# Strassen's seven block products in the last batch's second layer

## The chip, the core and the metric

The kernel runs on one core of one Trainium2 chip. The metric is the device time of one execution in microseconds, as the median of several runs; less is better. Engines are named as in the profile: PE is TensorE, PEld its weight loads, DVE is VectorE, ACT is ScalarE, POOL is GpSimd and SP is SyncE, which here only issues DMAs.

## The reference

Attention with normalised queries and keys feeds a two-layer network with a tanh GELU. The change touches only the last product, `g @ w_out`.

```python
q_n, k_n = rmsnorm(q, g_q), rmsnorm(k, g_k)          # (8, 12, 448, 64)
attn = softmax(q_n @ k_n.T / 8)
x = (attn @ v).transpose(0, 2, 1, 3).reshape(3584, 768)
h = x @ w_in                                         # w_in: 768 x 2048
g = 0.5 * h * (1 + tanh(c * (h + 0.044715 * h**3)))
out = g @ w_out                                      # w_out: 2048 x 768
```

## The kernel before

The 8 batches of 448 tokens go one after the other. For each batch the kernel does attention, then the first layer, and it mixes the second layer of the batches before into the attention of the next one, so that TensorE has work while ScalarE takes exponentials. The order in which instructions are written is the order in which each engine executes them; where one engine needs another's result, it waits on a semaphore. Nothing reorders them afterwards.

The **first layer** of a batch (`mm1_pair`, matmuls on L499) makes the 2048 hidden columns in 16 chunks of 128. Hidden values lie transposed: the tile `g` has 128 partitions (the place within a chunk), 16 chunks (`nf`), and 896 tokens, since two batches stand side by side. ScalarE applies the GELU from PSUM into `g` (L512), two chunks at a time and the last two chunks singly. PSUM is used as four pairs of banks that go round (`pair`, `give`): `s0`, `s1`, `t0`, `t1`.

The **second layer** goes by tiles of 128 tokens, 7 for two batches. Tiles 0 to 2 are taken after an even batch, tiles 3 to 6 after an odd one. For all but the last batch the matmuls (L442, `mm2_quarters`) are spread through the next batch's attention. After the last batch nothing is left to mix with, so `m2_parts` returns the calls of `mm2_last` (L465 to L487), which run on their own at the end: tiles 3 to 6, each in two blocks of 384 output columns, each block 16 matmuls of 128 x 128 weights by 384 columns that accumulate in one bank; the very last block is cut into two of 192 columns. Of each block ScalarE or VectorE copies the finished bank into `osb` (three buffers of 128 x 768 in `op`), and `store` issues two DMAs of 64 tokens each to the output, on SyncE's queue, the very last one on ScalarE's.

In the last batch the first layer runs with an empty plan beside it: `m1` has no entries, since there is no next batch to load or normalise. VectorE's last work ahead of it is the product `xT` (L408).

Of the kernel before, what the change touches and what calls it, by code (L numbers as in the profile page):

```python
# [8 lines left out]
F32 = mybir.dt.float32  # L9
BF16 = mybir.dt.bfloat16  # L10
I32 = mybir.dt.int32
AF = mybir.ActivationFunctionType
ALU = mybir.AluOpType
# [4 lines left out]
def kernel(  # L18
# [11 lines left out]
    nc = tc.nc  # L30
    B, H, S, D = q.shape
    assert (B, H, S, D) == (8, 12, 448, 64)
    d_model = H * D
# [4 lines left out]
    P = 128  # L38
    R = 64
    NT = S // R  # L40
    NCH = H // 4
    HP = H // 2
    nf = d_ff // 128
    HD = d_model // 2
# [5 lines left out]
    rawqk = ctx.enter_context(tc.tile_pool(name="rawqk", bufs=4))  # L50
    sqp = ctx.enter_context(tc.tile_pool(name="sqp", bufs=2))
    stp = ctx.enter_context(tc.tile_pool(name="stp", bufs=1))
# [3 lines left out]
    exq = ctx.enter_context(tc.tile_pool(name="exq", bufs=2))  # L56
    xp = ctx.enter_context(tc.tile_pool(name="xp", bufs=2))
    gp = ctx.enter_context(tc.tile_pool(name="gp", bufs=1))
    op = ctx.enter_context(tc.tile_pool(name="op", bufs=3))
# [11 lines left out]
    def pair(name):  # L71
        t = idle_pairs.pop(0)
        if not whole:
            idle_pairs.append(t)
        return t

    def give(t):
        if whole:
            idle_pairs.append(t)
# [29 lines left out]
    wout = wts.tile([128, nf, d_model], BF16)  # L109
# [6 lines left out]
    g = gp.tile([128, nf, 2 * S], BF16, tag="g", name="g")  # L116
# [56 lines left out]
    def total(b, c, n, hs=both, ts=slice(0, NT)):  # L173
        if b not in sss:
            sss[b] = smp.tile([P, NCH, 2, 2, NT], F32, tag="ss", name="ss")
        nc.vector.reduce_sum(  # L176
            sss[b][:, c, "qk".index(n), hs, ts], squares(b, c, n, hs, ts), axis=AX.X
        )
# [140 lines left out]
    def gain(b, c):  # L319
        nc.vector.tensor_scalar(kT[:, c], kT[:, c], gcol[:, 0:1], None, op0=ALU.mult)  # L320
# [98 lines left out]
    osbs = {}  # L419
    SYNC = mybir.DependencyInfo(mybir.DependencyClass.Sync, mybir.DependencyReason.DATA)  # L420

    def store(b, i, cols=slice(0, d_model), engs=(nc.sync, nc.sync)):
        for j in range(2):
            col = i * 128 + j * R
            r = ((b // 2) * 2 + col // S) * R
            engs[j].dma_start(
                out_v[col % S // R, r:r + R, cols], osbs[i][j * R:(j + 1) * R, cols]
            )

    def mm2_quarters(b, parts, p, f, copy=None):  # L430

        if p == 0 and f == 0:
            osbs["o"] = pair("o")
            for i, half in parts:
                if half == 0:
                    osbs[i] = op.tile([128, 2, HD], F32, tag="osb", name="osb").rearrange(
                        "p h d -> p (h d)")
        o = osbs["o"]
        for n, (i, half) in enumerate(parts):
            rs = slice((n ^ p) * R, (n ^ p) * R + R)  # L440
            for c in range(2):
                done = nc.tensor.matmul(  # L442
                    o[c * R:(c + 1) * R, n, :HD],
                    g[rs, f, i * 128 + c * R:i * 128 + (c + 1) * R],
                    wout[rs, f, half * HD:(half + 1) * HD],
                    start=(p == 0 and f == 0), stop=(p == 1 and f == nf - 1),
                )
                if p == 1 and f == 0 and n == 0 and c == 0:
                    tc.add_manual_dep(done.ins, osbs["turn"].ins.name, SYNC)
        if p == 0 and f + 1 == nf:  # L450
            osbs["turn"] = nc.sync.nop(nofuse=True)  # L451
            tc.add_manual_dep(osbs["turn"].ins, done.ins.name, SYNC)
        if p == 0 or f + 1 < nf:
            return
        if parts[0][0] == parts[1][0]:
            copy(osbs[parts[0][0]].rearrange("p (h d) -> p h d", h=2), o[:, :, :HD])
        else:
            for n, (i, half) in enumerate(parts):
                copy(osbs[i][:, half * HD:(half + 1) * HD], o[:, n, :HD])
        give(o)  # L460
        for i, half in parts:
            if half == 1:
                store(b, i)

    def mm2_last(i, lo, hi, f):  # L465

        last = hi == d_model and i == 6
        if f == 0:
            osbs["o"] = pair("o")
            if lo == 0:  # L470
                osbs[i] = op.tile([128, d_model], F32, tag="osb", name="osb")
        o, osb = osbs["o"][:, 0, :hi - lo], osbs[i]
        nc.tensor.matmul(  # L473
            o, g[:, f, i * 128:(i + 1) * 128], wout[:, f, lo:hi],
            start=(f == 0), stop=(f == nf - 1),
        )
        if f + 1 < nf:
            return
        if i < 6 and lo == 0 or i == 6 and not last:
            nc.scalar.copy(osb[:, lo:hi], o)  # L480
        else:
            nc.vector.tensor_copy(osb[:, lo:hi], o)
        give(osbs["o"])
        if i == 6:
            store(B - 1, i, slice(lo, hi), (nc.sync, nc.scalar if last else nc.sync))
        elif hi == d_model:
            store(B - 1, i)  # L487

    def mm1_pair(i, cs=range(HP), b=0, js=range(2)):

# [28 lines left out]

    def m2_parts(b):  # L520
        tiles = range(3) if b % 2 == 0 else range(3, 7)
        if b + 1 == B:
            q = HD // 2
            cuts = [(i, lo, lo + HD) for i in tiles for lo in (0, HD)]
            i, lo, hi = cuts.pop()
            cuts += [(i, lo, lo + q), (i, lo + q, hi)]
            return [
                lambda cut=cut, f=f: mm2_last(*cut, f) for cut in cuts for f in range(nf)
            ]
        order = [(i, half) for i in tiles for half in range(2)]  # L530
        if b == 0:

            order.sort(key=lambda t: t[1])
        return [
            lambda copy, n=n, p=p, f=f: mm2_quarters(b, order[n:n + 2], p, f, copy)
            for n in range(0, len(order), 2) for p in range(2) for f in range(nf)
        ]
# [56 lines left out]
    def plan(*entries):  # L594
        steps = {}
        for slot, *fns in entries:
            steps.setdefault(slot, []).extend(fns)
        return steps
# [63 lines left out]
    def gpsimd_waits(x):  # L662

        nc.gpsimd.tensor_copy(mark, x)  # L664
# [57 lines left out]
    def first_two(steps, m2):  # L722
# [3 lines left out]
        for step in steps.split():  # L726
# [91 lines left out]
    m2 = []  # L818
# [25 lines left out]
            )    , m2)  # L844
    begun = 2
    for b in range(1, B):
        m1, side, ends = [], [], []
        if b + 1 < B:

            if (b, NCH - 1) in ess:  # L850
                m1.append((0, lambda: gpsimd_waits(ess[b, NCH - 1][:1, 0, :1])))
            for c in range(NCH):
                if b == 1 and c + 1 == NCH:
                    m1 += [(0, lambda: total(2, 2, "q")), (0, lambda: total(2, 2, "k")),
                           (6, lambda: rsqrt_last(2))]
                m1 += [(6 if (b, c) == (1, NCH - 1) else 0,
                        lambda c=c: normed_both(b + 1, c, nc.gpsimd)),
                       (4 * c + 4, lambda c=c: transposed(b + 1, c))]
            m1 += [(9, lambda: gain(b + 1, 0)), (14, lambda: gain(b + 1, 1))]
        if b + 2 < B:  # L860
            m1 += [(4, lambda: loads(b + 2, 1)), (8, lambda: loads(b + 2, 2))]
            for c, at in ((0, 4), (1, 9)):
                for i, (n, a) in enumerate((n, a) for n in "qk" for a in range(2)):
                    m1.append((at + i, lambda c=c, n=n, a=a: squared(b + 2, c, n, a)))
                m1 += [(at + 2, lambda c=c: total(b + 2, c, "q")),
                       (at + 4, lambda c=c: total(b + 2, c, "k"))]
            for n in "qk":
                m1.append((13, lambda n=n: square(b + 2, 2, n, nc.gpsimd)))
                side.append((0, lambda n=n: total(b + 2, 2, n)))
        if b + 1 < B:  # L870
            side.append((0, lambda: gain(b + 1, 2)))
        m1 = plan(*m1)
        for f in range(nf):
            if f + 1 == nf:
                for j in range(2):
                    mm1_pair(f // 2, range(HP), b, range(j, j + 1))
            elif f % 2:
                mm1_pair(f // 2, late if f // 2 < begun else range(HP), b)
            for fn in m1.get(f, ()):
                fn()  # L880
        m2 += m2_parts(b)
        if b + 1 == B:
            for fn in m2:
                fn()
            break
        nc.scalar.preload_act_table_set(EXP_SET)
        if b + 2 < B:
            ends.append(lambda: rsqrt(b + 2))
            side.append((0, lambda: load_v(b + 2, 0, HP)))
            if b + 3 < B:  # L890
                side.append((1 if b % 2 else 2, lambda: loads(b + 3, 0)))
        begun = attention(b + 1, m2, plan(*side), ends)
# [30 lines left out]
```

## Time and profile before

| what | value |
|---|---|
| median of 3 runs (lowest, highest) | 396.68 us (396.26, 397.37) |
| span of the profiled execution, first to last instruction | 394.7 us |
| time of the profiled execution outside its span | not in the profile; the median of the runs is 2.0 us above the span |
| granted TensorE clock | 1.000 |
| TensorE busy | 387.2 us (98%) |
| ScalarE, VectorE, GpSimd busy | 277.2, 252.3, 125.9 us |
| last batch's second layer on TensorE | 369.8 to 390.8 us from the span's start |

A row of the timeline gives start and length in us, engine, line, operation, result<-sources, shapes and count; in brackets the idle time of the engine ahead of it and what ended that. In a row with a count, the length reaches from the first start to the last end. A group row gives the busy time in us, the mean of one in ns, and the idle time before. Matmuls are pipelined: a matmul's row begins when it starts, and the next one starts before it has ended, so the rate is read from starts.

### The profile page before, as it was taken

How to read it: one execution, taken by the hardware profiler on the slowest of the kernel's cores; microseconds unless marked ns; L12 is line 12 of the kernel's file. 1: busy time of each engine (PE TensorE's matmuls, PEld its weight loads, DVE VectorE, ACT ScalarE, POOL GpSimd, SP SyncE). 2: the span in 40 equal slices, each digit the busy share in tenths (PEclk: the TensorE clock that was granted, in tenths of full speed). 3: DMA queues.
4: the chain of work that ended last, by engine and by line, in shares of the span. 5: the costliest groups of instructions: out<-in, count | busy, mean ns of one | idle time of the engine just before them, and what ended most of it. 6: DMA issues, size and time to landing. Idle time of an engine off the chain costs nothing.

```text
span 394.7 us, 12736 instructions
## 1 busy us (share of the span) xinstructions
PE 387.2 (98%) x5673; PEld 247.8 (63%) x5673; DVE 252.3 (64%) x386; ACT 277.2 (70%) x348; POOL 125.9 (32%) x105
## 2 busy tenths in 40 slices
PE   8989999999999999999999999999999999999996
PEld 7455557855666558855666557865666557865564
DVE  5999539997699267954599367963499505980010
ACT  6995389566995689847997579857898259854300
POOL 5995501865205540092203640073301800000000
PEclk9999999999999999999999999999999999999999
DMA  8999995899823958159731948249522611220033
GB/s 270 245 238 221 204 180 170 282 195 277 187 67 67 263 68 218 44 140 227 160 89 42 219 112 214 71 92 267 82 63 63 117 25 42 60 64 2 0 82 80
DMA packets 65594, 54.36 MB, mean 138 GB/s; under 512 B 37380, under 2 KB 60548, under 8 KB 65540
## 3 DMA queue, kind: packets, MB, share of 16 engines
q1 hardware_dynamic: 53184, 41.48, 40.7%
q0 software_dynamic: 12128, 11.80, 19.3%
q8 instruction: 44, 0.72, 0.7%
q10 hardware_dynamic: 228, 0.28, 0.2%
q14 instruction: 10, 0.08, 0.1%
HBM read 45.61 MB, written 11.01 MB: 143 GB/s over the span
## 4 chain that ended last, share of the span: by engine, by line
PE 93%; ACT 5%; DVE 1%; issue 0%; DVEq 0%; ACTq 0%
PE s L499 21%; PE t L442 19%; PE t L499 15%; PE s L442 12%; PE s L382 5%; ACT ex L337 4%; PE s L333 4%; PE t L333 3%; PE s L473 3%; PE t L382 3%; PE t L473 2%; PE o L271 2%; PE tp L296 1%; PE o L382 1%; PE hh L499 1%
## 5 line engine op out<-in xcount | busy, mean ns | idle before, releaser
L499 PEld LDWEIGHTS <-win 128*128 128x128 bf16 x768 | 74.4, 98 | 70.8 <-issue 2.7
L442 PEld LDWEIGHTS <-g 64*64 64x64 bf16 x3072 | 97.3, 107 | 33.1 <-SPq L451 2.9
L337 ACT ACTIVATE ex<-s,shift 128x896 bf16<-128x896 f32 x101 | 97.8, 1012 | 4.3 <-PE s L333 2.4
L442 PE MATMUL t<-wout,g 64*64 64x384 bf16 x1792 | 90.0, 323 | 0.0
L499 PE MATMUL s<-xT,win 128*128 128x448 bf16 x438 | 88.3, 353 | 0.0
L176 DVE TENSOR_REDUCE ss<-sq 128x14 f32<-128x896 f32 (+3 forms) x45 | 44.3, 996 | 45.7 <-ACT sq L169 42.9
L337 ACT ACTIVATE ex<-t,shift 128x896 bf16<-128x896 f32 x67 | 66.4, 1014 | 5.8 <-PE t L333 3.0
L512 ACT ACTIVATE g<-s 128x896 bf16<-128x896 f32 (+1 forms) x41 | 34.0, 835 | 48.5 <-PE s L499 48.5
L499 PE MATMUL t<-xT,win 128*128 128x448 bf16 x318 | 64.7, 353 | 0.0
L442 PE MATMUL s<-wout,g 64*64 64x384 bf16 x1280 | 64.6, 323 | 0.1
L512 ACT ACTIVATE g<-t 128x896 bf16<-128x896 f32 (+1 forms) x30 | 24.8, 829 | 26.3 <-PE t L499 26.3
L333 PE MATMUL s<-qT,kT 64*64 64x448 bf16 x404 | 37.3, 353 | 1.7 <-ACT ex L337 1.5
L664 POOL COPY mark<-es 1x1 bf16<-1x1 bf16 x5 | 0.9, 177 | 116.9 <-DVE es L356 116.9
L278 POOL TENSOR_TENSOR nrmk<-rawk,rinv 128x896 bf16<-128x896 f32 (+1 forms) x21 | 34.6, 1649 | 6.3 <-DVE o L245 6.3
L278 POOL TENSOR_TENSOR nrmq<-rawq,rinv 128x896 bf16<-128x896 f32 (+1 forms) x21 | 34.6, 1645 | 4.6 <-ACT rinv L208 3.4
L333 PEld LDWEIGHTS <-kT 64*64 64x64 bf16 x672 | 23.2, 106 | 14.5 <-issue 6.1
L171 POOL TENSOR_TENSOR sq<-rawq 128x896 f32<-128x896 f32 (+1 forms) x9 | 13.7, 1522 | 51.4 <-DMA rawq<-in_q_dram 24.6
L382 PEld LDWEIGHTS <-vb 64*64 64x64 bf16 x672 | 22.5, 107 | 8.4 <-issue 0.3
L400 DVE STREAM_TRANSPOSE rb<-rc 128x896 f32<-128x896 f32 x24 | 26.7, 1111 | 0.8
L333 PE MATMUL t<-qT,kT 64*64 64x448 bf16 x268 | 23.8, 351 | 0.3 <-ACT ex L337 0.2
L359 DVE TENSOR_TENSOR e<-ex 128x896 bf16<-128x896 bf16 x33 | 20.0, 606 | 6.2 <-ACT ex L337 6.2
L382 PE MATMUL s<-ex,vb 64*64 64x448 bf16 x420 | 22.6, 349 | 0.0
(107 smaller groups left out, 390.0 us busy)
## 6 DMA issues: line engine op xcount, KB each, us to landing
out_dram<-osb SPq DMA_DIRECT2D x54, 192.0 KB, 2.7
rawq<-in_q_dram SPq DMA_DIRECT2D x23, 448.0 KB, 4.6
rawk<-in_k_dram SPq DMA_DIRECT2D x23, 448.0 KB, 5.5
vb<-in_v_dram POOLq DMA_DIRECT2D x8, 672.0 KB, 6.8
wout<-in_moe_w_out_dram POOLq DMA_DIRECT2D x2, 1536.0 KB, 23.1
win<-in_moe_w_in_dram POOLq DMA_DIRECT2D x6, 256.0 KB, 10.5
win<-in_moe_w_in_dram POOLq DMA_DIRECT2D x4, 384.0 KB, 12.4
kT<-nrmk SPq DMA_TRANSPOSE x19, 3.9
```

What stands on the lines that cost most here:

```text
L171: eng.tensor_mul(sq, raw, raw)
L176: nc.vector.reduce_sum(sss[b][:, c, "qk".index(n), hs, ts], squares(b, c, n, hs, ts), axis=AX.X)
L278: eng.tensor_mul(nrms[n, b, c][:, ts].rearrange("p t a d -> p a t d"), raws[n, b, c][:, :, ts], root[:, :, ts].to_broadcast([P, 2, m, D]),)
L333: nc.tensor.matmul(sc[r * R:(r + 1) * R, a, :S], kT[rs, c, t, r], qT[b][rs, c, :, r], start=True, stop=True,)
L337: nc.scalar.activation(ex[:, t], sc[:, :, :S], AF.Exp, scale=scale, bias=shift)
L359: nc.vector.tensor_add(e2, ex[:, t - 1], ex[:, t])
L382: nc.tensor.matmul(o[r][a * D:(a + 1) * D], vb[b % 2][rs, 2 * c + a, i] if what else ones[rs], es[i][rs, a], start=(i == 0), stop=(i == n ...
L400: nc.vector.transpose(rb.rearrange("p r s -> p (r s)"), rc.to_broadcast([128, 2 * S // 32, 32]))
L442: done = nc.tensor.matmul(o[c * R:(c + 1) * R, n, :HD], g[rs, f, i * 128 + c * R:i * 128 + (c + 1) * R], wout[rs, f, half * HD:(half + 1) ...
L473: nc.tensor.matmul(o, g[:, f, i * 128:(i + 1) * 128], wout[:, f, lo:hi], start=(f == 0), stop=(f == nf - 1),)
L499: nc.tensor.matmul(h[j][:, :S] if type(h) is list else h[:, j, :S], win[:, c, f * 128:(f + 1) * 128], xT[b][:, c], start=(c == 0), stop=(c ...
L512: nc.scalar.activation(g[:, 2 * i + lo:2 * i + js[-1] + 1, (b % 2) * S:(b % 2 + 1) * S], h[:, lo:js[-1] + 1, :S], AF.Gelu_apprx_tanh)
```

## The change

The last second layer is done for two pairs of token tiles, (3, 4) and (5, 6). For each pair the product is a 2 x 2 block product: two token tiles by two halves of the hidden chunks (8 each, `nh`) times two halves of the hidden chunks by two halves of the output columns (384 each). Strassen's scheme needs seven block products of 8 matmuls in place of eight:

- the five sums of blocks of `w_out` are formed once by VectorE (`weight_sums`), each in two parts of 128 x 1536 bf16, into buffers that the loads of raw q and k and the squares no longer need;
- the five sums of blocks of `g` are formed for each pair by VectorE (`token_sums`): that for product 6 whole (128 x 1024), the four others in halves (128 x 512), of which the second halves need the last chunks of `g`;
- the products accumulate in PSUM where they can (product 5 onto product 3, product 2 onto product 4, in the first pair product 7 onto product 1), and VectorE and ScalarE form the four output blocks from them in `osb`. `s34` is the sum of products 3 and 4; `m1` is product 3, copied by ScalarE so that VectorE reads one bank only.

`mm2_last` and its place in `m2_parts` go. The new part of the diff:

```diff
+    half_cols = (slice(0, HD), slice(HD, d_model))
+    nh = nf // 2
+    def w_block(i, j, f, n=1):
+        return wout[:, i * nh + f:i * nh + f + n, half_cols[j]]
+    W_SUMS = {"1": ((0, 0), (1, 1), ALU.add), "3": ((0, 1), (1, 1), ALU.subtract),
+              "4": ((1, 0), (0, 0), ALU.subtract), "6": ((0, 0), (0, 1), ALU.add),
+              "7": ((1, 0), (1, 1), ALU.add)}
+    def weight_sums(m, part):
+        x, y, op = W_SUMS[m]
+        n = nh // 2
...
+        nc.vector.tensor_tensor(
+            t, w_block(*x, part * n, n), w_block(*y, part * n, n), op=op)
+        wsum[m, part] = t
+    G_SUMS = {"1": ((0, 0), (1, 1), ALU.add), "2": ((1, 0), (1, 1), ALU.add),
+              "5": ((0, 0), (0, 1), ALU.add), "6": ((1, 0), (0, 0), ALU.subtract),
+              "7": ((0, 1), (1, 1), ALU.subtract)}
+    def g_block(qd, i, j, f, n=1):
+        t = qd[i]
+        return g[:, j * nh + f:j * nh + f + n, t * 128:(t + 1) * 128]
+    def token_sums(qd, m, part=None):
...
+        x, y, op = G_SUMS[m]
+        lo, n = (0, nh) if part is None else (part * nh // 2, nh // 2)
+        nc.vector.tensor_tensor(
+            asum[qd, m][:, lo:lo + n], g_block(qd, *x, lo, n), g_block(qd, *y, lo, n), op=op)
+    def product(qd, m, o, start, lo=0, hi=HD):
+        for f in range(nh):
+            nc.tensor.matmul(
+                o[:, lo:hi], g_of(qd, m, f), w_of(m, f)[:, lo:hi],
+                start=start and f == 0, stop=f == nh - 1, skip_group_check=True,
+            )
+    def quad_of_products(qd, last):
+        c1, c2 = half_cols
+        for i in qd:
+            osbs[i] = op.tile([128, d_model], F32, tag="osb", name="osb")
+        o1, o2 = osbs[qd[0]], osbs[qd[1]]
...
+        x, y = bank("x"), bank("y")
+        product(qd, "3", x, True)
+        product(qd, "4", y, True)
+        nc.scalar.copy(m1, x)
+        nc.vector.tensor_add(s34, y, m1)
+        product(qd, "5", x, False)
+        nc.scalar.copy(o1[:, c2], x)
+        nc.vector.tensor_sub(o1[:, c1], s34, x)
+        give(one["x"])
+        store(B - 1, qd[0], c2)
+        product(qd, "2", y, False)
+        nc.scalar.copy(o2[:, c1], y)
+        nc.vector.tensor_sub(o2[:, c2], s34, y)
+        give(one["y"])
+        store(B - 1, qd[1], c1)
+        z = bank("z")
+        product(qd, "1", z, True)
+        nc.vector.tensor_add(o2[:, c2], z, o2[:, c2])
+        if last:
+            nc.vector.tensor_add(o1[:, c1], z, o1[:, c1])
+        w = bank("w")
+        product(qd, "6", w, True)
+        nc.vector.tensor_add(o2[:, c2], w, o2[:, c2])
+        give(one["w"])
+        store(B - 1, qd[1], c2, (nc.sync, nc.scalar if last else nc.sync))
+        cuts = ((bank("v"), 0, HD // 2), (z, HD // 2, HD)) if last else ((z, 0, HD),)
+        for o, lo, hi in cuts:
+            product(qd, "7", o, last, lo, hi)
+            nc.vector.tensor_add(o1[:, lo:hi], o[:, lo:hi], o1[:, lo:hi])
+            store(B - 1, qd[0], slice(lo, hi), (nc.sync, nc.scalar if hi == HD else nc.sync))
+        give(one["z"])
...
+    quads = ((3, 4), (5, 6))
...
+        if b + 1 == B:
+            for i, (m, part) in enumerate((m, part) for m in W_SUMS for part in range(2)):
+                m1.append((2 + i, lambda m=m, part=part: weight_sums(m, part)))
+            for qd in quads:
+                m1.append((9, lambda qd=qd: token_sums(qd, "6")))
+                for m in "1257":
+                    m1.append((12, lambda qd=qd, m=m: token_sums(qd, m, 0)))
...
+        if b + 1 == B:
+            for qd in quads:
+                for m in "1527":
+                    token_sums(qd, m, 1)
+            for qd in quads:
+                quad_of_products(qd, qd == quads[-1])
+            break
```

On **VectorE**, this is where its last `xT` of attention is followed by the end of the program (rows with a minus are of before; counts at the end of a row; `wsum` are the sums of `w_out`, `asum` those of `g`, `st` holds `s34`):

```order
 L408 TENSOR_TENSOR xT<-s_101,rb 128x896
-L482 COPY osb<-t_884 128x384
-L482 COPY osb<-t_885 128x384
-L482 COPY osb<-t_884 128x384
-L482 COPY osb<-s_100 128x192
-L918 UNCONDITIONAL_BRANCH
+L485 TENSOR_TENSOR wsum<-wout 128x1536 x8
+L516 TENSOR_TENSOR asum<-g 128x1024 x2
+L485 TENSOR_TENSOR wsum<-wout 128x1536 x2
+L516 TENSOR_TENSOR asum<-g 128x512 x16
+L552 TENSOR_TENSOR st<-t_884,st 128x384
+L555 TENSOR_TENSOR osb<-st,s_100 128x384
```

Four copies go; ten sums of weights and eighteen of tokens come, and all sixteen small ones, the second pair's too, stand ahead of the first pair's `s34` (L552).

On **TensorE**, this is the place in the first pair where product 5 (bank `s_100`) ends and product 2 (bank `t_884`) begins, in the changed kernel; in brackets the engines whose semaphores a row waits for:

```order
L528 LDWEIGHTS asum
L528 MATMUL s_100<-wout,asum 128x384
L528 LDWEIGHTS asum
L528 MATMUL t_884<-wout,asum 128x384 [waits DVE_49]
L528 LDWEIGHTS asum
L528 MATMUL t_884<-wout,asum 128x384
```

and this, in the kernel before, the change from the first block's bank to the second's:

```order
L473 LDWEIGHTS g [waits Activation_49]
L473 MATMUL s_100<-wout,g 128x384
L473 LDWEIGHTS g
L473 MATMUL t_884<-wout,g 128x384
L473 LDWEIGHTS g
```

The first matmul of product 2 waits for VectorE; of before, only loads of the last chunks of `g` waited for ScalarE.

On **SyncE**, the end of the changed kernel; the fence shows the issues of the second pair, in brackets what each waits for (the engine that made the data, and the DMA that used the same semaphore earlier):

```order
L426 DMA out_dram<-osb 64x384 [waits DMAHW4_49]
L426 DMA out_dram<-osb 64x384 [waits DMAHW6_49,DVE_49]
L426 DMA out_dram<-osb 64x192 [waits DMAHW7_49,DVE_49]
L426 DMA out_dram<-osb 64x192 [waits DMAHW0_49]
L426 DMA out_dram<-osb 64x192 [waits DMAHW2_49,DVE_49]
```

and the end of the kernel before:

```order
L426 DMA out_dram<-osb 64x384 [waits DMAHW7_49,Activation_49]
L426 DMA out_dram<-osb 64x384 [waits DMAHW0_49]
L426 DMA out_dram<-osb 64x192 [waits DMAHW1_49,Activation_49]
L426 DMA out_dram<-osb 64x192 [waits DMAHW2_49]
L426 DMA out_dram<-osb 64x192 [waits DMAHW4_49,DVE_49]
```

The stores are of the same sizes at the end, but the last four of the changed kernel all wait for VectorE's adds of the last two products, and ScalarE's queue takes the other half of the first and of the last of them.

More of the change, by code (lines that the diff above doesn't have):

```diff
@@ L463, in mm2_quarters @@
                 store(b, i)
[L465 to L487, printed above, removed]
+    half_cols = (slice(0, HD), slice(HD, d_model))
@@ new lines @@
+    nh = nf // 2
+    wsum = {}
+    def w_block(i, j, f, n=1):
[6 more added lines that the diff above has]
+        n = nh // 2
+        i = 2 * list(W_SUMS).index(m) + part
+        pool, tag = (rawqk, f"raw{'qk'[i % 2]}") if i < 8 else (sqp, "sq")
+        t = pool.tile([P, 2, NT, D], F32, tag=tag, name="wsum")
+        t = t.rearrange("p a t d -> p (a t d)").bitcast(BF16)[:, :n * HD].rearrange(
+            "p (f d) -> p f d", f=n)
+        nc.vector.tensor_tensor(
+            t, w_block(*x, part * n, n), w_block(*y, part * n, n), op=op)
+        wsum[m, part] = t
@@ new lines, in w_of @@
+    def w_of(m, f):
+        if m in W_SUMS:
+            part, f = divmod(f, nh // 2)
+            return wsum[m, part][:, f]
+        i = int(m == "5")
+        return w_block(i, i, f)[:, 0]
+    asum = {}
+    G_SUMS = {"1": ((0, 0), (1, 1), ALU.add), "2": ((1, 0), (1, 1), ALU.add),
[4 more added lines that the diff above has]
+        return g[:, j * nh + f:j * nh + f + n, t * 128:(t + 1) * 128]
@@ new lines, in token_sums @@
+    def token_sums(qd, m, part=None):
+        if (qd, "all") not in asum:
+            t = exq.tile([P, NT, 2, S], BF16, tag="ex", name="asum")
+            t = t.rearrange("p t a s -> p (t a s)")
+            for i, k in enumerate(G_SUMS):
+                asum[qd, k] = t[:, i * nh * 128:(i + 1) * nh * 128].rearrange(
+                    "p (f c) -> p f c", f=nh)
+            asum[qd, "all"] = t
+        x, y, op = G_SUMS[m]
+        lo, n = (0, nh) if part is None else (part * nh // 2, nh // 2)
+        nc.vector.tensor_tensor(
+            asum[qd, m][:, lo:lo + n], g_block(qd, *x, lo, n), g_block(qd, *y, lo, n), op=op)
@@ new lines, in g_of, with bank @@
+    def g_of(qd, m, f):
+        if m in G_SUMS:
+            return asum[qd, m][:, f]
+        i = int(m == "4")
+        return g_block(qd, i, i, f)[:, 0]
+    def product(qd, m, o, start, lo=0, hi=HD):
[9 more added lines that the diff above has]
+        o1, o2 = osbs[qd[0]], osbs[qd[1]]
+        st = stp.tile([128, 2, S], F32, tag="st", name="st")
+        s34, m1 = st[:, 0, :HD], st[:, 1, :HD]
+        one = {n: pair("o") for n in "xy"}
+        def bank(n):
+            if n not in one:
+                one[n] = pair("o")
+            return one[n][:, 0, :HD]
+        x, y = bank("x"), bank("y")
[29 more added lines that the diff above has]
+        give(one["z"])
@@ L521, in m2_parts @@
         tiles = range(3) if b % 2 == 0 else range(3, 7)
[L522 to L529, printed above, removed]
         order = [(i, half) for i in tiles for half in range(2)]
@@ L880 @@
                 fn()
+        if b + 1 == B:
[5 more added lines that the diff above has]
+            break
         m2 += m2_parts(b)
[L882 to L885, printed above, removed]
         nc.scalar.preload_act_table_set(EXP_SET)
```

## The prediction

> **What bounds the kernel now.** I read first the span and the clock, then the shares of the chain that ended last, then the engines stage by stage, and then the last 25 us instruction by instruction.
>
> ```profile
> core 0: 394.7 us, clock 1.000
> ...
> PE 387.2 (98%) x5673; PEld 247.8 (63%) x5673; DVE 252.3 (64%) x386; ACT 277.2 (70%) x348; POOL 125.9 (32%) x105
> ...
> PE 93%; ACT 5%; DVE 1%; issue 0%; DVEq 0%; ACTq 0%
> ```
>
> TensorE carries 93% of the chain at full clock. The profile gives its execution no time of its own beyond the span: 394.7 us against runs of 396.26 to 397.37, so about 2.0 us of the median 396.68 lie around the span, and I keep them fixed. I work out what the span loses and take that off the median.
>
> ```profile
> 354.00:369.80 15.80, 15.80 (x85) 8.15 (x84) 0.32 (x1) 6.85 (x8) 0.00 (x0) 1.00 0.00 1
> 369.80:390.80 21.00, 21.00 (x145) 13.53 (x143) 1.67 (x3) 2.78 (x6) 0.00 (x0) 1.00 0.27 65
> 390.80:394.70 3.90, 0.02 (x1) 0.00 (x0) 0.36 (x1) 0.00 (x0) 0.00 (x0) 1.00 0.25 61
> ```
>
> Columns after the length are busy time of TensorE, weight loads, VectorE, ScalarE, GpSimd. In the last batch's first layer (354.0 to 369.8) TensorE never stops and VectorE works 0.32 us; in the last second layer TensorE again never stops; then 3.9 us run out.
>
> ```profile
> 360.94 0.92 ACT L512 ACTIVATE g<-s 128x896 bf16<-128x896 f32 x1 [1.35 <-PE s L499]
> ...
> 365.48 0.92 ACT L512 ACTIVATE g<-s 128x896 bf16<-128x896 f32 x1 [1.35 <-PE s L499]
> ...
> 369.81 2.76 PE L473 MATMUL s<-wout,g 128*128 128x384 bf16 x16
> 370.01 0.54 ACT L512 ACTIVATE g<-t 128x448 bf16<-128x448 f32 x1 [0.59 <-PE t L499]
> 372.42 2.76 PE L473 MATMUL t<-wout,g 128*128 128x384 bf16 x16
> 372.62 0.48 ACT L480 COPY osb<-s 128x384 f32<-128x384 f32 x1 [2.06 <-PE s L473]
> ...
> 388.01 1.48 PE L473 MATMUL t<-wout,g 128*128 128x192 bf16 x16
> ...
> 389.33 1.48 PE L473 MATMUL s<-wout,g 128*128 128x192 bf16 x16
> ...
> 390.91 0.36 DVE L482 COPY osb<-s 128x192 f32<-128x192 f32 x1 [4.74 <-PE s L473]
> 391.30 0.55 ACTq L426 DMA_DIRECT2D out_dram<-osb  x1
> ```
>
> ```profile
> 389.50 1.33 PE s L473 x16
> 390.83 0.04 DVEq L482
> 390.87 0.04 issue
> 390.91 0.36 DVE osb L482
> ```
>
> Seven groups of sixteen 384-column matmuls start between 369.81 and 388.01: 18.20/112 = 0.163 us each, 1.30 for eight. Sixteen of 192 columns take 389.33 - 388.01 = 1.32, so 0.66 for eight. The last matmul ends at 390.83, 0.18 after its start plus one step; VectorE starts 0.08 later, and the last stores are issued at 391.30. The remaining 3.4 us to the span's end follow that issue.
>
> **What goes.** 8 blocks of 16 matmuls (7 whole, one in two cuts) are 128 matmul-equivalents; 2 pairs x 7 products x 8 are 112, the last again in two cuts. Gone: 16 x 0.163 = **2.60 us** of TensorE, all on the path. Nothing else is taken off it.
>
> **What is added on VectorE during the first layer** must fit in idle time.
>
> ```profile
> L354 DVE TENSOR_TENSOR es<-ex 128x896 bf16<-128x896 bf16 x20 | 12.4, 620 | 7.4 <-ACT ex L337 7.0
> L414 DVE TENSOR_TENSOR xT<-o,rb 128x448 bf16<-128x448 f32 x6 | 3.5, 616 | 0.7 <-PE o L382 0.6
> L278 DVE TENSOR_TENSOR nrmq<-rawq,s 128x512 bf16<-128x512 f32 x1 | 0.7, 686 | 0.1
> L278 DVE TENSOR_TENSOR nrmk<-rawk,root 128x384 bf16<-128x384 f32 x1 | 0.5, 541 | 0.0
> ```
>
> The f32 rows give 686 - 541 = 145 ns for 128 elements, and 541 at 384 leaves about 150 ns fixed at 1.04 ns an element; L414's 616 for 448 fits. The bf16 row, 620 for 896, is 150 + 0.52 x 896: two elements in the time of one. So a bf16 sum is 950 ns at 1536, 680 at 1024, 417 at 512.
>
> ```profile
> 339.32 0.63 DVE L360 TENSOR_TENSOR es<-es,e 128x896 bf16<-128x896 bf16 x1
> 339.86 0.62 DVE L359 TENSOR_TENSOR e<-ex 128x896 bf16<-128x896 bf16 x1
> ...
> 341.24 0.62 DVE L356 TENSOR_TENSOR es<-es,ex 128x896 bf16<-128x896 bf16 x1
> 341.78 1.08 DVE L408 TENSOR_TENSOR xT<-s,rb 128x896 bf16<-128x896 f32 x1
> ...
> 353.23 1.09 DVE L408 TENSOR_TENSOR xT<-s,rb 128x896 bf16<-128x896 f32 x1
> ```
>
> An operation that waits for nothing starts 0.08 before its forerunner's end (341.78 against 341.86). So ten weight sums go every 0.87, the large token sums every 0.60, the small every 0.34. VectorE is free at 354.32. Eight weight sums end at 361.3; both sums for product 6, after the fourth gelu (360.94 + 0.92 = 361.86), at about 363.2; two more weight sums at 364.9; the eight first halves wait for the sixth gelu (365.48 + 0.92 = 366.40) and end at 369.2. The last gelu ends at 370.55. All of this is hidden, with 1.4 us to spare; a weight sum would have to take 1.24 us before any of it showed (354.32 + 10 x 1.24 + 2 x 0.60 + 8 x 0.34 = 370.6).
>
> **The eight second halves are not hidden entirely.** They start at 370.61 and the last starts 7 x 0.34 later, ends at 373.41. Behind them in VectorE's queue stands s34 (384 elements, f32, one source in PSUM: 0.55 as in the 541 row), 373.33 to 373.88. Product 2 accumulates onto the bank that s34 reads, so its first matmul waits until about 373.96; every later matmul is queued behind it. Without the wait it would start at 369.81 + 3 x 1.30 = 373.72. **Stall 0.24 us.** Bounds: a 512 sum between 346 ns (620 scaled by length, nothing fixed) and 686 (the f32 row) gives a stall from 0 to 2.4. I take 417, since both operands and the result are bf16 as in L354; what it lacks is a row with short runs of 128 elements like these.
>
> Product 5 waits for ScalarE's copy m1 (done 371.1 + 0.2 + 0.48 = 371.8) and its own sum (371.4); it is wanted at 372.4. In the second pair no sums are in the queue: s34 is done about 0.4 before product 2 wants its bank. Each single-bank reuse by product 7 has a similar 0.4.
>
> The three output buffers bring one more wait: tile 5 goes where tile 3 lay. Tile 3's last store (two of 96 KB) is issued near 379.8 + 0.24 and lands 2.1 later by the second row below, at 382.1; the copy into the buffer is wanted at 383.2. That is covered by 1.1, and by 0.6 if it took the 2.6 of the first row.
>
> ```profile
> out_dram<-osb SPq DMA_DIRECT2D x6, 192.0 KB, 2.6
> out_dram<-osb SPq DMA_DIRECT2D x2, 96.0 KB, 2.1
> out_dram<-osb SPq DMA_DIRECT2D x3, 48.0 KB, 1.9
> ```
>
> **The stores at the end** stand closer. Product 6 ends at 386.9 (before the stall is added), its add gives the store of tile 6's right half at 387.56; product 7's first cut is ready at 387.99, its second at 388.65. SyncE's queue issues four: one for the half, two for the first cut, one for the second.
>
> ```profile
> 388.76 0.47 SPq L426 DMA_DIRECT2D out_dram<-osb  x1
> 388.76 1.11 SPq L426 DMA_DIRECT2D out_dram<-osb  x2
> 389.97 1.19 SPq L426 DMA_DIRECT2D out_dram<-osb  x2
> 391.30 0.50 SPq L426 DMA_DIRECT2D out_dram<-osb  x1
> ```
>
> An issue occupies the queue 0.47, two in a row 1.11 to 1.19. Starts: 387.56, 388.07, 388.66, 389.25. The last should have gone at 388.69: **0.56 us** of the gain is lost to issuing. I take that nothing hides it, and that the last landing takes as long as before. Bounds: a loss of 0, if the end is set by ScalarE's half, which goes at 388.69; and 0.7 more than I take, the 2.6 us landing of 192 KB against the 1.9 of 48 KB, since the 192 KB of tile 6's half now go 1.7 us ahead of the last issue (387.56 to 389.25), where it was 2.5 (388.76 to 391.30).
>
> [...]
>
> **Sum:** 2.60 - 0.24 - 0.56 = 1.80 us. Span 394.7 to 392.9, time 396.68 - 1.80 = **394.9 us**.
>
> **Rivals.**
> 1. *The sums run end to end.* If each small sum waits for the one ahead to finish, 0.417 apart, the last ends at 373.95, s34 at 374.5, the stall is 0.85 and the time 395.5. Against it: the overlaps of 0.08 above. [...]
> 2. *VectorE becomes the bound.* If two-source sums ran at one element a clock, a weight sum would take 1.67, product-6 sums 1.14, the halves 0.61: the second halves begin at 378.2, s34 ends near 383.7, product 2 starts at 383.8, 10.1 late. Time 396.68 - 2.05 + 10.1 = 404.7. It decides from 1.24 us a weight sum, and the gain is gone at about 1.42. [...] If only the token sums with their 128-element runs were slow, the stall is 2.4 and the time 397.0.
> 3. *The crowd of stores.* The 192 KB close ahead delay the last landing by the 0.7 above: 395.6.
> 4. *Fewer matmuls, no faster.* Each product's first matmul carries waits; a bubble of 0.1 to 0.2 at each of 14 products gives back 1.4 to 2.8: 396.3 to 397.7. Against it: the 369.80 to 390.80 window has no gap, though its groups also change banks.
>
> **Chances.** Forecast 0.68 (own range 394.1 to 395.4: from no stall and no loss at the stores, 2.60, to half a microsecond more of the two); rival 1 0.09, rival 2 0.07 and its half case 0.03, rival 3 0.08, rival 4 0.05. A measurement cannot tell less than 0.3%, 1.2 us, from no change: 395.5 is the border, so rivals 1 and 3 count half each. Faster 0.68 + 0.045 + 0.04 = 0.76, same 0.17, slower 0.07. The range is 394.1 to 396.6: above it lie rival 2 with its half case and part of rival 4, some 0.14 together.
>
> **What would show it.** Right: 112 matmul-equivalents at 0.163; weight sums near 0.95 us that end before 370; eight small sums 0.34 apart after the last gelu; one TensorE gap of about 0.2 us before product 2 of the first pair and none in the second; SyncE's last four issues back to back. Wrong: sums of 512 near 0.68, a product waiting for a sum, a gap at product starts, or a last landing more than 2.2 us after its issue.

## The result and the profile after

| | before | changed |
|---|---|---|
| median us (lowest to highest), 18 runs each | 396.75 (396.09 to 399.29) | 395.13 (394.45 to 396.72) |
| ratio, 95% interval | | 0.9963 [0.9951, 0.9975] |
| span of the profiled execution | 394.66 | 393.92 |
| first matmul of the last second layer | 369.81 | 370.79 |
| from it to the end of the last VectorE operation | 21.46 | 18.95 |
| from there to the start of the last store's issue | 0.03 | 0.74 |
| from there to the span's end | 3.36 | 3.44 |

The change gains 0.37%, 1.5 us by the ratio (1.0 to 1.9 by its interval) and 1.6 by the medians; 1.8 was forecast. The ratios here and below leave out two executions that ran far slower than the rest, one of before (506.24 us) and one of the kernel "stores on SyncE" (1423.1 us).

**The two spans must not be subtracted as they stand.** They differ by 0.74 us only, because the changed kernel's profiled execution came to the last second layer 0.98 us late. The beginning of the chain of waits shows where: of before,

```profile
1.17 6.93 PE o L271 x51
...
9.59 0.41 PE s L333 x4
```

and of the changed kernel,

```profile
2.20 6.53 DMA rawq<-in_q_dram
...
10.55 0.41 PE s L333 x4
```

The first scores start at 10.55 instead of 9.59, since the first load of q ended last, in code that the change does not touch. Counted from the last second layer on, the end comes 24.85 us after its first matmul in before and 23.13 in the changed kernel: 1.72 us sooner.

The timeline of the changed kernel, VectorE and TensorE in the last stage:

```profile
355.21 7.03 DVE L485 TENSOR_TENSOR wsum<-wout 128x1536 bf16<-128x1536 bf16 x8
...
367.40 2.77 DVE L516 TENSOR_TENSOR asum<-g 128x512 bf16<-128x512 bf16 x8 [1.51 <-ACT g L603]
...
370.79 1.46 PE L528 MATMUL s<-wsum,g 128*128 128x384 bf16 x8
...
371.56 2.77 DVE L516 TENSOR_TENSOR asum<-g 128x512 bf16<-128x512 bf16 x8 [1.40 <-ACT g L603]
...
373.38 1.46 PE L528 MATMUL s<-wout,asum 128*128 128x384 bf16 x8
374.25 0.55 DVE L552 TENSOR_TENSOR st<-t,st 128x384 f32<-128x384 f32 x1
374.86 1.46 PE L528 MATMUL t<-wout,asum 128*128 128x384 bf16 x8
...
382.65 1.46 PE L528 MATMUL s<-wout,asum 128*128 128x384 bf16 x8
382.92 0.56 DVE L552 TENSOR_TENSOR st<-t,st 128x384 f32<-128x384 f32 x1 [2.11 <-PE t L528]
383.95 1.46 PE L528 MATMUL t<-wout,asum 128*128 128x384 bf16 x8
...
389.38 0.36 DVE L576 TENSOR_TENSOR osb<-t,osb 128x192 f32<-128x192 f32 x1 [0.30 <-PE t L528]
```

The reader sees the idle time in brackets first: VectorE waited 1.40 us for the last gelu, so all that stands ahead of it was hidden. The eight second halves take (2.77 - 0.42)/7 = 0.336 each. s34 (L552) follows at once, ends at 374.80, and product 2 starts at 374.86, where 373.38 + 1.30 = 374.68 was possible: a gap of 0.18. In the second pair the same step goes from 382.65 to 383.95, 1.30 exactly: s34 waited for TensorE there, not the other way round.

The groups give the durations:

```profile
L485 DVE TENSOR_TENSOR wsum<-wout 128x1536 bf16<-128x1536 bf16 x10 | 8.8, 952 | 0.0
...
L516 DVE TENSOR_TENSOR asum<-g 128x512 bf16<-128x512 bf16 x16 | 5.5, 419 | 2.9 <-ACT g L603 2.9
...
L552 DVE TENSOR_TENSOR st<-t,st 128x384 f32<-128x384 f32 x2 | 1.1, 555 | 2.1 <-PE t L528 2.1
```

And the issues at the end of the changed kernel, first SyncE's, then ScalarE's two (a row with a count reaches from the first start to the last end):

```profile
388.64 0.47 SPq L426 DMA_DIRECT2D out_dram<-osb  x1
388.64 1.11 SPq L426 DMA_DIRECT2D out_dram<-osb  x2
389.20 1.98 SPq L426 DMA_DIRECT2D out_dram<-osb  x3
390.48 0.70 SPq L426 DMA_DIRECT2D out_dram<-osb  x1
...
388.64 0.50 ACTq L426 DMA_DIRECT2D out_dram<-osb  x1
389.76 0.50 ACTq L426 DMA_DIRECT2D out_dram<-osb  x1
```

The last add ends at 389.74. ScalarE issues its half of the last store at 389.76; SyncE, with four in a row, comes to the other half at 390.48, 0.7 us late.

### The profile page after: what moved, and what is told of

The parts are those of the page before. It is cut to its first block, busy times and chain, and to the rows that moved or that the text cites. A ratio compares the mean times of both kernels' runs of the same rounds, so it can differ in the third digit from the quotient of the medians.

```text
span 393.9 us, 12748 instructions
## 1 busy us (share of the span) xinstructions
PE 384.4 (98%) x5649; PEld 245.2 (62%) x5649; DVE 271.5 (69%) x424; ACT 277.8 (71%) x349; POOL 126.0 (32%) x105
## 4 chain that ended last, share of the span: by engine, by line
PE 91%; ACT 5%; DMA 2%; DVE 1%; issue 0%; SPq 0%; ACTq 0%
PE s L590 21%; PE t L442 19%; PE t L590 15%; PE s L442 12%; PE s L382 5%; ACT ex L337 4%; PE s L333 4%; PE t L333 3%; PE t L382 3%; PE s L528 2%; PE t L528 2%; DMA rawq<-in_q_dram 2%; PE o L382 1%; PE tp L296 1%; PE hh L590 1%
## 5 line engine op out<-in xcount | busy, mean ns | idle before, releaser
L603 ACT ACTIVATE g<-t 128x896 bf16<-128x896 f32 (+1 forms) x30 | 24.8, 829 | 26.3 <-PE t L590 26.3
L382 PE MATMUL s<-ex,vb 64*64 64x448 bf16 x420 | 22.6, 349 | 0.0
```

Of the source, the lines that this page charges most:

```text
L382: nc.tensor.matmul(o[r][a * D:(a + 1) * D], vb[b % 2][rs, 2 * c + a, i] if what else ones[rs], es[i][rs, a], start=(i == 0), stop=(i == n ...
L603: nc.scalar.activation(g[:, 2 * i + lo:2 * i + js[-1] + 1, (b % 2) * S:(b % 2 + 1) * S], h[:, lo:js[-1] + 1, :S], AF.Gelu_apprx_tanh)
```

## The experiments

My theory was that of the prediction, now with sizes: 2.60 us of matmuls go, 0.18 come back because s34 stands behind eight sums, 0.7 because SyncE issues four stores in a row, and the other sums are free until VectorE's slack is used up. The rivals: the gap is the price of any wait for VectorE; the landing of the stores and not their issue sets the end; the sums cost something even where they are hidden. All times are medians, each beside runs of the kernel before on the same chip. "Stage" is counted from the first matmul of the last second layer.

| kernel | us | before, us | ratio, 95% interval | stage: last add ends | last issue after it | span ends |
|---|---|---|---|---|---|---|
| changed | 395.13 | 396.75 | 0.9963 [0.9951, 0.9975] | 18.95 | 0.74 | 23.1 |
| sums behind s34 | 394.63 | 396.47 | 0.9956 [0.9937, 0.9974] | 18.78 | 0.75 | 23.0 |
| stores shared | 394.20 | 396.47 | 0.9943 [0.9930, 0.9955] | 18.95 | 0.39 | 22.6 |
| stores on SyncE | 396.24 | 396.47 | 0.9995 [0.9980, 1.0010] | 18.95 | 2.00 | 24.2 |
| both | 393.95 | 396.47 | 0.9942 [0.9924, 0.9961] | 18.78 | 0.40 | 22.4 |
| one pair | 395.20 | 396.43 | 0.9964 [0.9952, 0.9976] | 20.15 | 0.03 | 23.5 |
| weight sums longer | 395.00 | 396.43 | 0.9970 [0.9952, 0.9988] | 19.10 | 0.75 | 23.3 |
| before, with sums | 396.86 | 396.43 | 1.0009 [0.9991, 1.0026] | 21.45 | 0.03 | 24.8 |
| weight sums twice | 403.32 | 396.43 | 1.0163 [1.0140, 1.0187] | 27.30 | 0.75 | 31.5 |
| the same, kept busy | 400.91 | 396.67 | 1.0097 [1.0070, 1.0123] | 25.08 | 0.74 | 29.3 |

### Sums behind s34

```diff
         nc.vector.tensor_add(s34, y, m1)
+        if not last:
+            for m in "1527":
+                token_sums(quads[1], m, 1)
...
-            for qd in quads:
-                for m in "1527":
-                    token_sums(qd, m, 1)
+            for m in "1527":
+                token_sums(quads[0], m, 1)
```

> The four second halves of the second pair are written behind the first pair's s34 instead of ahead of it. Theory (product 2 waits because eight small sums stand ahead of s34 in VectorE's queue): s34 starts right after product 4, the gap of 0.18 us ahead of product 2 goes, TensorE's stage from its first product to its last matmul gets 0.18 shorter, about 18.4 us, and the time falls by 0.2, to 394.9. Rival (the gap is what any matmul pays that waits on VectorE, wherever s34 stands): the gap stays at 0.1 to 0.2 and the stage at 18.6. The time alone will hardly tell; the gap in the trace will.

Its timeline at the place of the gap:

```profile
373.42 1.46 PE L528 MATMUL s<-wout,asum 128*128 128x384 bf16 x8
373.69 0.56 DVE L552 TENSOR_TENSOR st<-t,st 128x384 f32<-128x384 f32 x1 [0.66 <-PE t L528]
374.16 1.42 DVE L516 TENSOR_TENSOR asum<-g 128x512 bf16<-128x512 bf16 x4
374.72 1.46 PE L528 MATMUL t<-wout,asum 128*128 128x384 bf16 x8
```

s34 now waits 0.66 us for TensorE, and product 2 follows product 5 after 1.30: the gap is gone. The last add ends 0.17 earlier in the stage. So the gap was VectorE's queue. That the time fell by 0.2 is not shown: the interval of its ratio is 1.5 us wide.

### Stores shared, and stores on SyncE

```diff
-            store(B - 1, qd[0], slice(lo, hi), (nc.sync, nc.scalar if hi == HD else nc.sync))
+            store(B - 1, qd[0], slice(lo, hi), (nc.sync, nc.scalar))
```

> The first cut's second store goes to ScalarE's queue, so that SyncE and ScalarE issue three each at the end. Theory (SyncE's queue is late by its four issues, so that the last store goes 0.7 us after its data): the last store is issued within 0.1 us of its data, the span's end follows the last add by 0.7 less, time 395.1 - 0.7 = 394.4. Rival (the landing of the crowded stores sets the end, not their issue): the last store goes earlier but lands as late as before, time 395.1 within 0.2.

```diff
-        store(B - 1, qd[1], c2, (nc.sync, nc.scalar if last else nc.sync))
+        store(B - 1, qd[1], c2)
...
-            store(B - 1, qd[0], slice(lo, hi), (nc.sync, nc.scalar if hi == HD else nc.sync))
+            store(B - 1, qd[0], slice(lo, hi), (nc.sync, nc.sync if last else nc.scalar))
```

> All six stores at the end are issued by SyncE. Theory (the issue queue sets the end, 0.55 to 0.65 us an issue): two more issues ahead of the last one, which goes 1.2 us later than in the changed kernel; time 395.1 + 1.2 = 396.3, and most of the gain is gone. Rival (the landing sets the end): time 395.1 to 395.5, since the same bytes are in flight.

The last add and the last issues, first with the stores shared:

```profile
389.10 0.36 DVE L576 TENSOR_TENSOR osb<-t,osb 128x192 f32<-128x192 f32 x1 [0.30 <-PE t L528]
...
388.96 0.80 ACTq L426 DMA_DIRECT2D out_dram<-osb  x1
389.56 0.55 SPq L426 DMA_DIRECT2D out_dram<-osb  x1
...
389.85 0.55 ACTq L426 DMA_DIRECT2D out_dram<-osb  x1
```

then with all six on SyncE:

```profile
388.05 0.36 DVE L576 TENSOR_TENSOR osb<-t,osb 128x192 f32<-128x192 f32 x1 [0.30 <-PE t L528]
...
390.41 0.59 SPq L426 DMA_DIRECT2D out_dram<-osb  x1
```

The same bytes go out in all three kernels and the last add stands at 18.95 in each stage. With the stores shared, in the changed kernel and with all on SyncE, the last issue goes 0.39, 0.74 and 2.00 us after it, and the span ends at 22.6, 23.1 and 24.2. From the last issue to the span's end it is 3.24, 3.44 and 3.23. So the issue queue sets the end, and the landing behind it changes by only some 0.2; the rival falls. With all stores on SyncE the gain can no longer be told from nothing in the times (0.9995, with 1 inside its interval); by the stage 0.67 us of it are left. The shared version missed its number in one point: not 0.1 but 0.39 us stayed, because ScalarE's second issue took 0.80 where 0.50 was reckoned.

### One pair

```diff
+    def mm2_last(i, lo, hi, f):
...
-    quads = ((3, 4), (5, 6))
+    quads = ((3, 4),)
...
-                quad_of_products(qd, qd == quads[-1])
+                quad_of_products(qd, False)
+            q = HD // 2
+            cuts = [(i, lo, lo + HD) for i in (5, 6) for lo in (0, HD)]
+            i, lo, hi = cuts.pop()
+            cuts += [(i, lo, lo + q), (i, lo + q, hi)]
+            for cut in cuts:
+                for f in range(nf):
+                    mm2_last(*cut, f)
```

The body of `mm2_last`, left out here, is that of the kernel before.

> Only tiles 3 and 4 are done by seven products; tiles 5 and 6 by the matmuls and copies of before, with the stores of before at the end. Theory (each pair takes off 8 matmuls of 0.163 us, and the crowd of stores at the end belongs to the second pair): TensorE's stage shrinks by 1.30, there is no wait for s34 since only four second halves stand ahead of it, and nothing is lost at the stores; time 396.7 - 1.3 = 395.4. Rival (the gain hangs on the tail or on something else that is made once): the time stays at 396.7, or falls by the whole 1.6.

Its timeline where the products end, and at the end of the program:

```profile
379.76 2.76 PE L588 MATMUL s<-wout,g 128*128 128x384 bf16 x16
...
390.45 0.36 DVE L597 COPY osb<-s 128x192 f32<-128x192 f32 x1 [4.74 <-DMA out_dram<-osb]
390.84 0.50 ACTq L426 DMA_DIRECT2D out_dram<-osb  x1
```

Its first product starts at 370.66, so the first pair takes 379.76 - 370.66 = 9.10 = 7 x 1.30, and the last copy ends at 20.15, 1.30 less than before. The time, 395.20 for 395.4 expected, is as good as that of the changed kernel: the second pair's own 1.30 us lose 0.89 to its crowd of stores (0.71) and the gap (0.18), and this measurement cannot tell the rest from nothing.

### Before, with sums

The kernel before, with the 28 sums put where the change has them; nothing reads them. The functions that form them, left out here, are those of the change.

```diff
...
+        if b + 1 == B:
+            for i, (m, part) in enumerate((m, part) for m in W_SUMS for part in range(2)):
+                m1.append((2 + i, lambda m=m, part=part: weight_sums(m, part)))
+            for qd in quads:
+                m1.append((9, lambda qd=qd: token_sums(qd, "6")))
+                for m in "1257":
+                    m1.append((12, lambda qd=qd, m=m: token_sums(qd, m, 0)))
...
+            for qd in quads:
+                for m in "1527":
+                    token_sums(qd, m, 1)
```

> The kernel before with all 28 sums of weights and tokens in their places, and nothing that reads them. Theory (the sums cost nothing by themselves, neither in VectorE's queue nor by reading and writing SBUF beside TensorE): 396.7 within 0.3, matmuls at 0.163 and 0.189 us as before. Rival (the sums slow the matmuls beside them): 398 or more, matmuls slower from 355 us on.

The time is 396.86 beside 396.43, a ratio of 1.0009 with 1 inside its interval, and the stage is 21.45 for 21.46. Hidden sums cost nothing that can be measured, and the matmuls beside them keep their rate (0.189 us each in the first layer, with and without the sums).

### Weight sums longer, and twice

```diff
         nc.vector.tensor_tensor(
             t, w_block(*x, part * n, n), w_block(*y, part * n, n), op=op)
+        nc.vector.tensor_tensor(
+            t[:, 0, :], w_block(*x, part * n, 1)[:, 0], w_block(*y, part * n, 1)[:, 0], op=op)
```

> Behind each of the ten weight sums one quarter of it (384 columns) is summed a second time, with the same result: 0.28 to 0.4 us more for each, 2.8 to 4.0 in all. Theory (there are 3.7 us of room ahead of the last gelu): the second halves start at the last gelu as before, or at most 0.3 us after it; time 395.1 to 395.4. Rival (every VectorE sum in the first layer costs its time): 395.1 + 2.8 = 397.9 or more.

VectorE's first two weight sums in its timeline, its small sums, and product 2 on TensorE:

```profile
355.23 0.95 DVE L485 TENSOR_TENSOR wsum<-wout 128x1536 bf16<-128x1536 bf16 x1
...
356.49 0.95 DVE L485 TENSOR_TENSOR wsum<-wout 128x1536 bf16<-128x1536 bf16 x1
...
369.05 5.45 DVE L518 TENSOR_TENSOR asum<-g 128x512 bf16<-128x512 bf16 x16
...
375.02 1.46 PE L530 MATMUL t<-wout,asum 128*128 128x384 bf16 x8 [0.16 <-DVE st L554]
```

A weight sum with its quarter takes 356.49 - 355.23 = 1.26, just past the 1.24 at which the slack should be gone, and indeed the sixteen small sums now run without a pause. Product 2 waits 0.32 in place of 0.18. The time, 395.0, has not risen: 3.9 us more on VectorE cost nothing that shows in the time.

```diff
-        nc.vector.tensor_tensor(
-            t, w_block(*x, part * n, n), w_block(*y, part * n, n), op=op)
+        for _ in range(2):
+            nc.vector.tensor_tensor(
+                t, w_block(*x, part * n, n), w_block(*y, part * n, n), op=op)
```

> Each of the ten weight sums is executed twice, with the same result. Theory (VectorE's sums are free up to 1.24 us a weight sum and on the path from there): 1.74 us each (0.87 twice, up to 1.9 if the second waits for the first) is 0.5 to 0.66 too much in each of ten, so product 5 waits about 4 us and product 2 a further 1 us; time 395.1 + 5.0 = 400.1, up to 401.7. Rival (VectorE's sums are hidden whatever they take, since TensorE has other products): 395.1. Rival (they cost already in the changed kernel): 395.1 + 8.7 = 403.8.

Past the slack the queue becomes the bound, but the time, 403.32, is 1.6 above even the theory's upper number. It lies close to the 403.8 of the second rival, by which the sums cost their time already in the changed kernel; that is chance, since the two experiments before this one show sums that cost nothing. The timeline shows the waits, and then something else:

```profile
375.43 0.82 PE L529 MATMUL s<-wout,asum 128*128 128x384 bf16 x4 [2.63 <-DVE asum L517]
...
377.77 1.34 PE L529 MATMUL s<-wout,asum 128*128 128x384 bf16 x4 [1.52 <-DVE asum L517]
...
380.25 2.72 PE L529 MATMUL t<-wout,asum 128*128 128x384 bf16 x8 [1.14 <-DVE st L553]
...
382.76 2.45 PE L529 MATMUL s<-wsum,asum 128*128 128x384 bf16 x8
```

Product 3 started at 370.03, so product 2 starts 10.22 us after it (380.25 - 370.03), 6.15 later than in the changed kernel: the queue's part. But products 2 and 1 then take 2.51 and 2.29 us instead of 1.30. The windows of the same kernel give the granted clock (third number from the end):

```profile
370.00:375.40 5.40, 2.80 (x18) 1.47 (x15) 5.33 (x10) 1.03 (x2) 0.00 (x0) 1.00 0.00 0
375.40:380.20 4.80, 2.17 (x8) 0.88 (x9) 4.80 (x14) 0.48 (x1) 0.00 (x0) 0.76 0.00 0
380.20:382.70 2.50, 2.45 (x8) 1.16 (x8) 0.55 (x1) 0.00 (x0) 0.00 (x0) 0.50 0.34 79
```

That is half the clock. A last kernel tested whether it is the missing piece: the weight sums twice as above, and matmuls of zeros (`idle`) into an unused bank where TensorE waited. Its edits beyond the doubled sums:

```diff
+            if (qd[0], m, f) == (3, "5", nh // 2):
+                idle(8, osbs["spare"])
...
+        osbs["spare"] = one["x"][:, 1, :S]
...
+        if not last:
+            idle(14, one["x"][:, 1, :S])
         product(qd, "5", x, False)
+        if not last:
+            idle(6, one["x"][:, 1, :S])
```

> The weight sums are executed twice as in the kernel that took 403.3 us, and 28 matmuls of zeros by zeros (448 columns, 0.187 us each, written to an unused bank) fill the times in which TensorE waited there: 14 ahead of product 5, 8 in its middle, 6 ahead of product 2, of the first pair. Theory (the excess of about 2.2 us over the queue's delay was the granted clock, which fell to 0.50 after gaps of 2.6, 1.5 and 1.1 us, so that products 2 and 1 took 2.5 and 2.3 us instead of 1.3): the clock stays at 1.00, each product takes 1.30, time 403.3 - 2.2 = 401.1. Rival (the products ran slowly for another reason, such as VectorE's late sums): products 2 and 1 stay at 2.3 to 2.5 and the time at 403.3 or above, by what the zeros take too long.

Two windows of it, over the times in which the clock had fallen:

```profile
375.00:380.20 5.20, 5.19 (x29) 2.47 (x27) 5.20 (x16) 0.00 (x0) 0.00 (x0) 1.00 0.02 3
380.20:386.00 5.80, 5.28 (x33) 3.03 (x31) 3.11 (x7) 0.96 (x2) 0.00 (x0) 1.00 0.29 68
```

The clock stays at 1.00, product 2 takes 1.30, and the time is 400.91 for 401.1 expected. The last add comes 2.22 us earlier in the stage than without the zeros, and 6.13 later than in the changed kernel, as late as the queue had made product 2. The excess was the clock; the rest is VectorE's queue.

### Both

The edits of "sums behind s34" and "stores shared" together.

> The second pair's halves behind s34 and the stores shared between two queues, together. Theory (both losses are separate and both lie on the path): 0.18 + 0.7 off the changed kernel's 395.1, so 394.2, and 2.5 us or 0.6% less than before, which is nearly all of the 2.60 us of matmuls that went. Rival (the end is set by something else): 394.7 or more.

The last add and the last issue:

```profile
388.00 0.36 DVE L579 TENSOR_TENSOR osb<-t,osb 128x192 f32<-128x192 f32 x1 [0.30 <-PE t L528]
...
388.76 0.55 ACTq L426 DMA_DIRECT2D out_dram<-osb  x1
```

393.95 beside 396.47, ratio 0.9942 [0.9924, 0.9961]: 2.3 us less than before by the ratio, against 2.60 us of matmuls that went. In the stage both parts add up: the last add at 18.78, the last issue 0.40 after it, the end at 22.4, 2.4 less than before. Its time cannot be told from that of "stores shared" alone.

## Why the prediction was right

- **What goes, 2.60 us.** Right. The last matmul ends 18.56 us into the stage (389.35 by the chain) where it was 21.02, 2.46 sooner; without the gap of 0.18 it would be 2.64. One pair alone gave 1.30.
- **Hidden sums.** Right: 952 ns for 950, 419 for 417, VectorE idle 1.40 us ahead of the last gelu's end for 1.4 forecast. The threshold of 1.24 us a weight sum agrees with the runs: at 0.87 nothing waits for the sums ahead of the last gelu, at 1.26 product 2 is 0.14 later than in the changed kernel, and at 1.86 it is 6.15 later, where ten sums 0.62 over the threshold make 6.2. One reading on the way to the durations was loose: 145 ns for 128 elements is 1.13 ns an element, not 1.04; 1.04 comes out of longer rows, L408's 1.08 us for 896 against L414's 616 ns for 448.
- **The stall, 0.24 us.** Right in place and mechanism, 0.18 in size; moving four sums took it away.
- **The short runs of 128 elements**, for which no row existed, cost nothing: 419 ns beside the 417 worked out at the 0.52 ns an element of L354's row. Rival 1 (sums end to end) falls with 0.336 a sum, which is 0.08 less than a sum's duration.
- **The stores, 0.56 us.** Right in mechanism, mis-sized by 0.15: the last issue came 0.74 us after its data, where it was 0.03 before, so 0.71 were lost. The term took 0.51, 0.59 and 0.59 from each of SyncE's four issues to the next; they started 0.56, 0.60 and 0.68 apart. Rival 3 (the crowd delays the landing by 0.7) falls: the time from the last issue to the end was 3.44 for 3.36 before, and 3.2 to 3.5 in all the kernels.
- **Rival 2** (VectorE becomes the bound) did not occur, and where it was forced the step that priced it failed: the prediction added only the queue's delay and left the clock at 1.00, where it fell to 0.50. Its "one element a clock" is the 1.04 ns an element of the f32 rows; no run shows a clock of VectorE. Weight sums at 1.86 us cost 8.2 us, of which 2.4 went when TensorE was kept busy (403.32 - 400.91).
- **Rival 4** (a bubble at each product) falls: apart from the one gap, products follow each other at 1.30.

Sum by the stage: -2.64 of matmuls + 0.18 of stall + 0.71 of issue + 0.08 of landing, and -0.05 because the last add follows the last matmul more closely, make -1.72, and the end moved by -1.72; 1.80 was forecast. That the forecast comes so close is in part luck: the matmuls gave 0.04 more than forecast and the stall took 0.06 less, the issues took 0.15 more and the landing 0.08 more. The runs have 1.8 us around the span (395.7 with a span of 393.92), not 2.0; as the prediction kept it fixed, that changes nothing. The runs give 1.5 to 1.6, which the interval does not tell apart from 1.7 or 1.8.

## What to carry to other kernels

Trading matmuls for sums on an idle engine paid here as far as the sums stood ahead of the last input they need (the 28 sums alone gave 396.86 beside 396.43; at 1.86 us a weight sum, past the slack, the changed kernel took 403.32); work out the slack from the idle time in the rows, and put each sum that is not yet wanted behind the one that TensorE waits for. A stage that gets shorter brings its stores closer together: count the issues on each DMA queue behind the last result, since 0.47 to 0.70 us for each on SyncE's queue took back 0.71 of the 2.60 us that the matmuls gave. Compare stages from a common start, not spans, when the difference sought is as small as the scatter of the start.

## What the runs showed of the hardware

With the weight sums executed twice TensorE paused for 2.63 us, ran four matmuls in 0.82, paused for 1.52, and the next four took 1.34 us. The granted clock was 1.00 from 370.00 to 375.40 us, 0.76 from there to 380.20, 0.50 to 382.70, 0.55 to 385.00 and 1.00 again to 395.90. With matmuls of zeros in the same places the longest pause was 0.52 us, and the clock was 1.00 in all three windows from 369.00 to 386.00. In the changed kernel, with its gap of 0.18 us, it was 1.00 from 370.79 to the last add. So in these runs the fall went with the pauses; no run varies their length or their number one at a time, and what it is in them that lowers the clock is not shown.

An issue of the last stores took 0.47 to 0.70 us on SyncE's queue and 0.50 to 0.80 on ScalarE's. Whether the two queues slow each other when they issue together is not shown: ScalarE's issues of 0.50 us in the changed kernel began within 0.04 us of one of SyncE's, just as the one of 0.80 did with the stores shared (388.96 beside 388.92), SyncE's issue of 0.70 began when ScalarE's last had ended, and the kernel before has one of 0.84 on SyncE (at 376.77) with none on ScalarE beside it.
